# Routing attention and a tanh-shrink feed-forward: scores as [key, query], two heads on two halves of the array, masks by codes

## The chip, the core and the metric

One core of a Trainium2 chip. The metric is device time in microseconds of one execution of the program, from the first to the last instruction; of several runs the median counts.

## The reference

There are 4 batches, 8 heads, 768 tokens and 64 dimensions per head. Each token of q and of k is given one of 16 clusters of its head, and a query attends only to the keys of its own cluster. The attention's output, [3072 tokens, 512], goes through an up-projection to 2048, h - tanh(h), and a down-projection to 512.

```python
q_assign = np.argmax(np.einsum('bhsd,hcd->bhsc', q_n, c_n), axis=-1)   # k_assign alike
mask = q_assign[:, :, :, None] == k_assign[:, :, None, :]
scores = scale * np.matmul(q, k.transpose(0, 1, 3, 2))
scores = np.where(mask, scores, -1000000000.0)
scores = scores - np.max(scores, axis=-1, keepdims=True)
attn = np.exp(scores)
attn = attn / (np.sum(attn, axis=-1, keepdims=True) + 1e-09)
x = np.matmul(attn, v)            # then heads side by side: (3072, 512)
h = x @ w_in
out = (h - np.tanh(h)) @ w_out
```

q, k, v and the centroids are float32 normals times 0.1. The two weights come as float64 and are rounded to float32 on the chip. All arithmetic is float32.

## The kernel before

The 32 heads (4 batches x 8) are worked on one after the other, g = 0 to 31. The 768 tokens of a head stand as 6 chunks of 128 partitions.

For one head, `turn` (L185) transposes q and k from [token, d] to [d, token] on TensorE, 12 transposes `pt`. `route` (L201) multiplies each chunk with the 16 centroids (`pr`, 12 thin products of 16 columns), takes the argmax on VectorE as a one-hot row, transposes it (`po`) and puts it under the turned q, and (one-hot - 1) x 2^60 under the turned k. So one product over 64 + 16 rows gives the masked score: `score` (L237) does it for one chunk of 128 queries against 768 keys, two products of 384 columns. `softmax` (L245) takes the row's maximum on VectorE (L248), the exponential with its sum on ScalarE (L251), and scales by the reciprocal on VectorE (L256). `turn_weights` (L258) transposes the 128x768 weights in six 128x128 transposes (`pw`, L267) and ScalarE copies them out (L269). `values` (L271) multiplies v with the turned weights of half a head's queries, six products `av` (L279), into rows 0 to 63 or 64 to 127 of `xT` by the head's parity.

The projections (`ffn_items`, L287) work on half a batch, 384 tokens. There are 16 items `up` (four products `h` of 384 columns, L296, a tanh on ScalarE, L301, and a subtraction `g` on VectorE, L302) and 12 items `project` (four products `o` of 512 columns, L308). The items of a finished batch are spread over the next batch's eight heads by `step` in the main loop: they are issued between a head's chunks. Those of the last batch follow at the end. A float32 product is issued as two instructions of TensorE, each with a weight load of its own; a transpose is one instruction.

Weights are loaded in 32 pieces by GpSimd's queue (L111) and rounded by six VectorE operations and one GpSimd addition each (L115 to L134), four pieces per head of batch 0. Loads of q, k and v are on SP's queue (L183), two heads ahead, with 1536 bytes in a row per partition. The centroids' load (L147) is the fourth on that queue. The output's stores are on GpSimd's queue (L315).

The order on each engine is that of a scheduler, which starts from the order in which the program issues the work. PSUM has eight banks: two score tiles of two banks (`ps_s`), two for transposes (`ps_t`), two for `av`, `h` and `o` (`ps_f`).

Of the kernel before, what the change touches and what calls it, by code (L numbers as in the profile page):

```python
# [26 lines left out]
BF16 = mybir.dt.bfloat16  # L27
U32 = mybir.dt.uint32
# [7 lines left out]
TINY = 1e-30  # L36


@with_exitstack
def kernel(  # L40
# [11 lines left out]
    PSUM = bass.MemoryType.PSUM  # L52

# [5 lines left out]
    NG = B * H  # L59
    KR = D + C  # L60
# [7 lines left out]
    assert H * C == P and 2 * D == P and H * D == DM  # L68

    const = ctx.enter_context(tc.tile_pool(name="const", bufs=1))  # L70
    loads = ctx.enter_context(tc.tile_pool(name="loads", bufs=3))
    xtp = ctx.enter_context(tc.tile_pool(name="xtp", bufs=2))
    rtp = ctx.enter_context(tc.tile_pool(name="rtp", bufs=2))
    expp = ctx.enter_context(tc.tile_pool(name="expp", bufs=3))
# [26 lines left out]
    def load_weights(n: int):  # L101
# [4 lines left out]
        if words == 1:  # L106
            nc.gpsimd.dma_start(dst, src)
            return
# [30 lines left out]
    def constants():  # L139
        make_identity(nc, ident)  # L140
        nc.vector.tensor_copy(out=identb, in_=ident)
        for c in range(C):
            nc.vector.memset(down[:, c : c + 1], float(C - c))
# [216 lines left out]
    for it in fill:  # L360
        it()
# [31 lines left out]
```

## Time and profile before

| | |
|---|---|
| median of three runs | 1651.25 us (1644.41 to 1651.29) |
| span of the profiled execution | 1650.8 us |
| TensorE busy | 1565.0 us, 95% |
| VectorE / ScalarE / GpSimd busy | 702.1 / 464.0 / 78.5 us |
| products and transposes of TensorE, busy | `o` 362.1, `h` 357.5, `sc` 311.1, `av` 276.4, `pw` 173.5, `pr` 101.7, `pt` 54.8, `po` 32.3 us |

The engines work in parallel, and busy time is each engine's own. The span is the profiled execution from its first to its last instruction; runs are timed without the profiler. A matmul's recorded duration contains its way through the array, which overlaps the next one's, so the pace of a group is read from the start of the group to the start of the next. The granted clock is the share of 2.4 GHz that TensorE was given over a stretch; its two levels are 1.2 and 2.4 GHz.

### The profile page before, as it was taken

What the parts mean: (1) busy time and instruction counts of PE and PEld (TensorE: products, weight loads), DVE (VectorE), ACT (ScalarE), POOL (GpSimd) and SP (SyncE); (2) the same over time, 40 slices, a digit from 0 to 9 for tenths busy, and PEclk for the clock granted to TensorE, in tenths of its full rate; (3) what the DMA queues carried; (4) which work ended last, traced back from release to release, by engine and by line L of the source; (5) the groups of instructions that cost most, each with busy time, mean ns of one, the idle gap of its engine ahead of it and who ended that gap; (6) DMA issues with size and microseconds to landing.
All of it is one profiled execution on the core that took longest, in us unless ns stands there. A gap on an engine that the chain in (4) does not pass through costs nothing.

```text
span 1650.8 us, 15280 instructions
## 1 busy us (share of the span) xinstructions
PE 1565.0 (95%) x6017; PEld 880.4 (53%) x6017; DVE 702.1 (43%) x1463; ACT 464.0 (28%) x995; POOL 78.5 (5%) x94
## 2 busy tenths in 40 slices
PE   4788788899999999999999999999999999999998
PEld 2444445556555555555555555556655566545453
DVE  6857675544433444334433444334443344321010
ACT  1223333433322333223322333223322233221010
POOL 3312220000000000000000000000000000000000
PEclk9877787989999999999999999999999999999999
DMA  4212210000000000000000000000000000000000
GB/s 169 90 55 74 70 53 15 29 15 15 15 17 11 22 15 15 24 24 15 12 10 21 21 15 15 21 27 3 13 15 27 21 15 1 7 13 0 19 0 19
DMA packets 20567, 42.96 MB, mean 26 GB/s; under 512 B 2576, under 2 KB 14864, under 8 KB 20496
## 3 DMA queue, kind: packets, MB, share of 16 engines
q0 software_dynamic: 6528, 23.07, 4.2%
q1 hardware_dynamic: 13968, 18.91, 3.7%
q8 instruction: 48, 0.79, 0.2%
q14 instruction: 23, 0.19, 0.0%
HBM read 35.68 MB, written 6.29 MB: 25 GB/s over the span
## 4 chain that ended last, share of the span: by engine, by line
issue 70%; PE 19%; DVE 7%; ACT 2%; POOL 1%; DMA 0%; POOLq 0%; ACTq 0%
PE av L279 5%; PE sc L240 4%; PE pw L267 3%; PE pr L206 3%; PE h L296 3%; DVE raw L130 1%; PE o L308 1%; DVE top L248 1%; ACT e L251 1%; POOL out_dram L315 1%; ACT eT L269 1%; DVE rest L126 1%; PE po L225 1%; PE pt L192 1%; DVE e L256 0%
## 5 line engine op out<-in xcount | busy, mean ns | idle before, releaser
L308 PE MATMUL o<-w_out,g 128*128 128x512 f32 x768 | 362.1, 619 | 0.0
L296 PE MATMUL h<-xT,w_in 128*128 128x384 f32 x1024 | 357.5, 495 | 0.0
L240 PE MATMUL sc<-xqk 80*128 80x384 f32 x768 | 311.1, 518 | 19.4 <-ACT e L251 18.1
L251 ACT ACTIVATE e<-sc,top 128x768 f32<-128x768 f32 x192 | 173.1, 902 | 483.5 <-DVE top L248 478.1
L279 PE MATMUL av<-eT,x 128*64 128x384 f32 x768 | 276.4, 511 | 0.9 <-ACT eT L269 0.2
L296 PEld LDWEIGHTS h<-xT,w_in 128*128 128x128 f32 x1024 | 193.1, 193 | 128.7 <-issue 6.6
L248 DVE TENSOR_REDUCE top<-sc 128x1 f32<-128x768 f32 x192 | 183.2, 956 | 144.1 <-PE sc L240 144.0
L308 PEld LDWEIGHTS o<-w_out,g 128*128 128x128 f32 x768 | 147.3, 196 | 163.4 <-issue 151.6
L269 ACT COPY eT<-pw 128x384 f32<-128x384 f32 x384 | 167.2, 483 | 216.6 <-PE pw L267 216.0
L267 PEld LDWEIGHTS pw<-ident,e 128*128 128x128 f32 x1152 | 142.8, 148 | 101.5 <-issue 58.8
L279 PEld LDWEIGHTS av<-eT,x 128*64 128x64 f32 x768 | 103.5, 142 | 161.4 <-issue 127.3
L267 PE MATMUL pw<-ident,e 128*128 128x128 f32 x1152 | 173.5, 288 | 14.8 <-DVE xqk L199 4.7
L240 PEld LDWEIGHTS sc<-xqk 80*128 80x128 f32 x768 | 133.0, 199 | 101.7 <-issue 41.4
L282 DVE COPY xT<-av 64x384 f32<-64x384 f32 x64 | 35.5, 555 | 295.2 <-PE av L279 295.1
L301 ACT ACTIVATE th<-h 128x384 f32<-128x384 f32 x128 | 63.1, 493 | 253.0 <-PE h L296 250.4
L256 DVE TENSOR_SCALAR e<-e,rec 128x768 f32<-128x768 f32 x192 | 121.0, 630 | 5.7
L302 DVE TENSOR_TENSOR g<-h,th 128x384 f32<-128x384 f32 x128 | 71.4, 558 | 118.3 <-ACT th L301 110.9
L206 PEld LDWEIGHTS pr<-cnT,xqk 64*128 64x128 f32 x768 | 98.5, 206 | 18.6 <-ACT eT L269 18.2
L206 PE MATMUL pr<-cnT,xqk 64*128 64x16 f32 x768 | 101.7, 275 | 1.5 <-ACT eT L269 1.5
L315 POOL DMA_DIRECT2D out_dram<-osb x24 | 13.0, 544 | 1372.3 <-DVE osb L314 1372.3
L228 ACT CAST xqk<-po 16x768 f32<-16x768 bf16 x32 | 25.3, 790 | 162.6 <-PE po L225 162.6
L253 DVE TENSOR_SCALAR den<-total 128x1 f32<-128x1 f32 x192 | 29.0, 151 | 89.6 <-ACT e L251 84.6
(52 smaller groups left out, 581.0 us busy)
## 6 DMA issues: line engine op xcount, KB each, us to landing
raw<-in_moe_w_in_dram POOLq DMA_DIRECT2D x16, 512.0 KB, 4.7
raw<-in_moe_w_out_dram POOLq DMA_DIRECT2D x16, 512.0 KB, 3.9
x<-in_q_dram SPq DMA_DIRECT2D x32, 192.0 KB, 2.4
x<-in_k_dram SPq DMA_DIRECT2D x32, 192.0 KB, 2.5
x<-in_v_dram SPq DMA_DIRECT2D x32, 192.0 KB, 3.1
out_dram<-osb POOLq DMA_DIRECT2D x24, 256.0 KB, 2.3
cen<-in_centroids_dram SPq DMA_DIRECT2D x1, 32.0 KB, 6.3
```

What stands on the lines that cost most here:

```text
L206: nc.tensor.matmul(pr[:, j], lhsT=x[0:D, j], rhs=cnT[:, g % H], start=True, stop=True)
L240: nc.tensor.matmul(sc[:, half, 0:TB], lhsT=xqk[g][:, 0, i], rhs=xqk[g][:, 1, half * HCH : (half + 1) * HCH], start=True, stop=True,)
L248: nc.vector.tensor_reduce(out=top, in_=sc, axis=AX.XY, op=ALU.max, negate=True)
L251: nc.scalar.activation(out=e, in_=sc, func=ACT.Exp, bias=top, scale=1.0, accum_out=total)
L256: nc.vector.tensor_scalar_mul(out=e, in0=e, scalar1=rec)
L267: nc.tensor.transpose(out=pt[:, j], in_=e[:, c * P : (c + 1) * P], identity=ident)
L269: nc.scalar.copy(out=dst, in_=pt)
L279: nc.tensor.matmul(av[r], lhsT=x32[g][:, 2, j], rhs=eT[:, j], start=(j == 0), stop=(j == NCH - 1))
L296: nc.tensor.matmul(h, lhsT=w_in[i][:, c, o * P : (o + 1) * P], rhs=xT[b][:, c, half * TB : (half + 1) * TB], start=(c == 0), stop=(c == CD ...
L301: nc.scalar.activation(out=th, in_=h, func=ACT.Tanh)
L302: nc.vector.tensor_tensor(out=gs[i][:, o], in0=h, in1=th, op=ALU.subtract)
L308: nc.tensor.matmul(acc[sub], lhsT=gs[i][:, o, sub * P : (sub + 1) * P], rhs=w_out[i][:, o], start=(i == 0 and o == 0), stop=(i == NQ4 - 1 ...
```

## The change

The kernel's working part is rewritten as `fast()`, issued under a schedule written by hand (`tc.manual_schedule()`), so that each engine's order is the program's.

- Heads go in pairs (16 pairs). q and k of two heads are loaded side by side, [128, 6, 2, 64], so each transpose turns both heads: head 0 lands on partitions 0 to 63, head 1 on 64 to 127.
- `similar` multiplies both heads with a block-diagonal of their centroids (32 columns), four products of 384 columns into four strips of 32 partitions; `route` turns the result in three transposes and finds each token's code (16 minus its cluster's number) by four VectorE operations; `publish` turns the queries' codes to rows and stores them in DRAM; `spread` loads them back onto all 128 partitions.
- `score` gives [key, query] for one chunk of 128 keys and 384 queries of both heads: two products of 64 rows, head 0 on rows 0 to 63, head 1 on 64 to 127, into two PSUM banks. ScalarE takes the exponential in place, without a maximum. `select` on VectorE multiplies it with (query's code == key's code), which gives the weights as [key, query], with nothing to turn.
- `value` multiplies v with the weights, head 0 into output partitions 0 to 63, head 1 into 64 to 127. GpSimd adds the weights up, `total` sums them over the keys by a product with ones, and `divide` takes reciprocals and scales.
- A step is two key chunks of a pair and half of the queries; a pair and half has three steps, a block (half a batch) four pairs, twelve steps; there are eight blocks. The projections of block n - 1 are issued among the steps of block n, 28 items over 12 steps, those of block 7 at the end. Block 0 has none. One piece of weights is rounded per step in block 0 and three per step in block 1, with four VectorE operations, one on ScalarE and one on GpSimd.
- If any sum of weights lies outside 2^-5 to 2^80, a flag sends the program on to `general()`, which computes everything again as before, without overlap. It is left out below.
- The output's copies move from VectorE to ScalarE and its stores from GpSimd's queue to SP's.

```diff
...
+    def fast():
...
+        loads = cx.enter_context(tc.tile_pool(name="loads", bufs=2))
+        vp = cx.enter_context(tc.tile_pool(name="vp", bufs=4))
+        codep = cx.enter_context(tc.tile_pool(name="codep", bufs=5))
+        qbp = cx.enter_context(tc.tile_pool(name="qbp", bufs=3))
+        ep = cx.enter_context(tc.tile_pool(name="ep", bufs=2))
+        ps_s = cx.enter_context(tc.tile_pool(name="ps_s", bufs=2, space=PSUM))
+        ps_a = cx.enter_context(tc.tile_pool(name="ps_a", bufs=2, space=PSUM))
+        ps_f = cx.enter_context(tc.tile_pool(name="ps_f", bufs=2, space=PSUM))
...
+        def round_weights(n: int):
...
+            nc.scalar.activation(out=rest, in_=lo, func=ACT.Copy, scale=2.0**-29)
...
+            nc.gpsimd.tensor_tensor(out=rest, in0=bits, in1=rest, op=ALU.add)
+            nc.vector.tensor_scalar(
+                out=bits, in0=hi, scalar1=20, scalar2=0x7FF,
+                op0=ALU.logical_shift_right, op1=ALU.bitwise_and,
+            )
+            nc.vector.scalar_tensor_tensor(
+                out=dst, in0=bits, scalar=float(F32_LEAST), in1=rest.bitcast(F32),
+                op0=ALU.is_ge, op1=ALU.mult,
+            )
...
+        def load(n: int, what=(0, 1)):
...
+                for h in range(2):
+                    nc.sync.dma_start(
+                        t[:, :, h], (q, k, v)[i][b, 2 * p + h].rearrange("(p j) d -> p j d", p=P)
+                    )
+        def turn(n: int):
+            for i in range(2):
+                pt = ps_s.tile([P, 2, 512], F32, name="pt", tag="s")
+                x = raw_qk.pop((n, i))
+                for j in range(NCH):
+                    nc.tensor.transpose(
+                        out=pt[:, j // HCH, (j % HCH) * P : (j % HCH + 1) * P],
+                        in_=x[:, j].rearrange("p h d -> p (h d)"), identity=ident,
+                    )
...
+        def similar(n: int):
+            for i in range(2):
+                for half in range(2):
+                    r = (2 * i + half) * 2 * C
+                    nc.tensor.matmul(
+                        ps[r : r + 2 * C, 0, 0:TB], lhsT=bd[:, pairs[n][1]],
+                        rhs=turned[n, i][:, half], start=True, stop=True, tile_position=(0, r),
+                    )
+            t = rtp.tile([P, TB], F32, name="simt")
+            nc.scalar.copy(out=t, in_=ps[:, 0, 0:TB])
...
+        def route(n: int):
+            ps, t = sims.pop(n)
+            for j in range(HCH):
+                nc.tensor.transpose(
+                    out=ps[:, 1, j * P : (j + 1) * P], in_=t[:, j * P : (j + 1) * P], identity=ident
+                )
...
+            nc.vector.reduce_max(out=mx, in_=pr, axis=AX.X)
...
+            nc.vector.tensor_tensor(out=top, in0=top, in1=places, op=ALU.mult)
+            code = codes[n] = codep.tile([P, 2, 2, 2, HCH], F32, name="code")
+            nc.vector.reduce_max(
+                out=code.rearrange("p i a h j -> p j (i a h)"),
+                in_=top.rearrange("p (j g) c -> p j g c", j=HCH), axis=AX.X,
+            )
...
+        def publish(n: int):
+            ps, code = sims.pop(n)
+            G = HCH * 4
+            nc.tensor.transpose(
+                out=ps[0:G, 0, 0:P], in_=code[:, 0].rearrange("p a h j -> p (a h j)"), identity=ident
+            )
+            t = rtp.tile([G, P], F32, name="qc")
+            nc.vector.tensor_copy(out=t, in_=ps[0:G, 0, 0:P])
+            q_codes[n] = dram.tile([2, 2, HCH, P], F32, name="q_codes")
+            nc.sync.dma_start(q_codes[n].rearrange("a h j p -> (a h j) p"), t)
+        rows = {}
+        def spread(n: int, half: int):
+            t = rows[n, half] = qbp.tile([P, 2, TB], F32, name="row")
+            nc.sync.dma_start(
+                t.rearrange("p h n -> p (h n)"),
+                q_codes[n][half].rearrange("h j p -> (h j p)").unsqueeze(0).to_broadcast([P, 2 * TB]),
+            )
+        def score(n: int, half: int, j: int):
+            sc = scores[n, half, j] = ps_s.tile([P, 2, 512], F32, name="sc", tag="s")
+            for h in range(2):
+                r = slice(h * D, h * D + D)
+                nc.tensor.matmul(
+                    sc[:, h, 0:TB],
+                    lhsT=turned[n, 1][r].rearrange("p a n -> p (a n)")[:, j * P : (j + 1) * P],
+                    rhs=turned[n, 0][r, half], start=True, stop=True,
+                )
+            nc.scalar.activation(out=sc[:, :, 0:TB], in_=sc[:, :, 0:TB], func=ACT.Exp, scale=SCALE)
+        def select(n: int, half: int, j: int):
+            if j % 2 == 0:
+                weights[n, half, j // 2] = ep.tile([P, 2, 2, TB], F32, name="e")
+            e = weights[n, half, j // 2][:, j % 2]
+            sc = scores.pop((n, half, j))
+            for h in range(2):
+                nc.vector.scalar_tensor_tensor(
+                    out=e[:, h], in0=rows[n, half][:, h],
+                    scalar=codes[n][:, 1, j // HCH, h, j % HCH : j % HCH + 1], in1=sc[:, h, 0:TB],
+                    op0=ALU.is_equal, op1=ALU.mult,
+                )
+            if j % 2 == 1:
+                pair = weights[n, half, j // 2]
+                if j == 1:
+                    s = sums[n, half] = sump.tile([P, 2, TB], F32, name="sum")
+                    nc.gpsimd.tensor_tensor(out=s, in0=pair[:, 0], in1=pair[:, 1], op=ALU.add)
+                else:
+                    s = sums[n, half]
+                    for i in range(2):
+                        nc.gpsimd.tensor_tensor(out=s, in0=s, in1=pair[:, i], op=ALU.add)
+        def value(n: int, half: int, s: int):
+            e = weights.pop((n, half, s))
+            if s == 0:
+                avs[n, half] = ps_a.tile([P, TB], F32, name="av", tag="a")
+            for i in range(2):
+                j = 2 * s + i
+                for h in range(2):
+                    nc.tensor.matmul(
+                        avs[n, half][h * D : h * D + D], lhsT=vals[n][:, j, h], rhs=e[:, i, h],
+                        start=(j == 0), stop=(j == NCH - 1),
+                    )
+        dens = {}
+        def total(n: int, half: int):
+            b, p = pairs[n]
+            s = sums.pop((n, half))
+            ps = ps_a.tile([P, TB], F32, name="den", tag="a")
+            for h in range(2):
+                nc.tensor.matmul(
+                    ps[h * D : h * D + D], lhsT=ones, rhs=s[:, h], start=True, stop=True
+                )
+            if p == 0:
+                xT[b, half] = xp.tile([P, CD, TB], F32, name="xT")
+            nc.scalar.copy(out=xT[b, half][:, p], in_=avs.pop((n, half)))
+            t = dens[n, half] = sump.tile([P, TB], F32, name="den")
+            nc.scalar.activation(out=t, in_=ps, func=ACT.Copy, bias=EPS)
+            is_in = okp.tile([P, TB], F32, name="is_in")
+            for bound, op in ((SUM_LEAST, ALU.is_ge), (SUM_MOST, ALU.is_le)):
+                nc.gpsimd.tensor_scalar(out=is_in, in0=t, scalar1=bound, scalar2=None, op0=op)
+                nc.gpsimd.tensor_tensor(out=ok, in0=ok, in1=is_in, op=ALU.mult)
+        def divide(n: int, half: int, part: int):
+            b, p = pairs[n]
+            c = slice(part * P, (part + 1) * P)
+            t = dens[n, half]
+            nc.vector.reciprocal(out=t[:, c], in_=t[:, c])
+            if part == HCH - 1:
+                x = xT[b, half][:, p]
+                nc.vector.tensor_tensor(out=x, in0=x, in1=dens.pop((n, half)), op=ALU.mult)
...
+        load(0)
+        constants()
+        load(0, (2,))
+        load(1)
+        for n in range(1, HP):
+            load(n, (2,))
+        centroid_norms()
+        for n in range(2):
+            fetch_weights(n)
+        fetched, rounded = 2, 0
...
+        def prepare(n: int, stage: int):
+            if n >= len(pairs):
+                return
+            if stage == 0:
+                turn(n)
+                load(n + 2)
+            elif stage == 1:
+                similar(n)
+            elif stage == 2:
+                route(n)
+            elif stage == 3:
+                publish(n)
+                spread(n, 0)
+        for stage in range(4):
+            prepare(0, stage)
+        begin(steps[0])
+        for i in range(2):
+            select(*steps[0][:2], i)
+        fill, late = [], []
+        for at, (n, half, s) in enumerate(steps):
+            b, p = pairs[n]
+            following = steps[at + 1] if at + 1 < len(steps) else None
+            if p == 0 and s == 0:
+                block = 2 * b + half
+                fill = ffn_items((block - 1) // 2, (block - 1) % 2) if block else []
+            left = HP * NS - (p * NS + s)
+            now = [fill.pop(0) for _ in range(-(-len(fill) // left))]
+            nxt = n + 1 if half == 0 and p + 1 < HP else (b + 1) * HP if half == 1 and p + 1 == HP else None
+            if nxt is not None and s == NS - 1:
+                prepare(nxt, 3)
+            if following:
+                begin(following)
+            value(n, half, s)
+            if s == NS - 1:
+                total(n, half)
+                late += [lambda n=n, half=half, i=i: divide(n, half, i) for i in range(HCH)]
+                if half == 1:
+                    load(n + HP, (2,))
+            todo = []
+            if following:
+                todo += [lambda i=i: select(*following[:2], 2 * following[2] + i) for i in range(2)]
+            todo += late
+            late = []
+            if block <= 1:
+                todo += [weights_on] * (1 if block == 0 else 3)
+            pre = [lambda: None] * 4
+            if nxt is not None:
+                pre = [lambda st=st: prepare(nxt, st) for st in range(4)]
+            if half == 1 or (half == 0 and p == HP - 1):
+                m = b * HP + p + 1 if half == 1 and p + 1 < HP else b * HP if half == 0 else None
+                if m is not None and s == 0:
+                    spread(m, 1)
+            slots = max(len(now), 1)
+            for i in range(slots):
+                mine = todo[i * len(todo) // slots : (i + 1) * len(todo) // slots]
+                def between(mine=mine):
+                    for it in mine:
+                        it()
+                if i < len(now):
+                    now[i](between)
+                else:
+                    between()
+                if i == max(slots - 2, 0):
+                    if s == 0:
+                        pre[0]()
+                    elif s == 1:
+                        pre[1]()
+                if i == slots - 1 and s == 1:
+                    pre[2]()
+        fill = ffn_items(B - 1, 1)
+        for it in late:
+            it()
+        for it in fill:
+            it(lambda: None)
...
+    fine = nc.values_load(flag[0:1, 0:1], min_val=0, max_val=1)
+    with tc.If(fine < 1):
+        with ExitStack() as cx:
+            general()
```

## Rows read from the trace of the kernel before

**Rows 1.** The page's list of busy time.
```profile
PE 1565.0 (95%) x6017; PEld 880.4 (53%) x6017; DVE 702.1 (43%) x1463; ACT 464.0 (28%) x995; POOL 78.5 (5%) x94
```

**Rows 2.** Stretches: us; PE, PEld, DVE, ACT, POOL busy; clock, DMA share, GB/s.
```profile
0.00:20.00 20.00, 6.14 (x28) 4.66 (x28) 8.12 (x40) 2.45 (x4) 5.52 (x13) 1.00 0.69 240
38.10:358.00 319.90, 264.14 (x1056) 154.26 (x1057) 211.58 (x440) 101.01 (x216) 53.01 (x50) 0.80 0.17 53
100.00:200.00 100.00, 79.41 (x307) 47.28 (x306) 67.25 (x143) 28.07 (x60) 22.03 (x22) 0.74 0.22 65
455.00:1475.00 1020.00, 1019.76 (x4030) 570.81 (x4028) 400.37 (x825) 305.33 (x659) 9.79 (x18) 0.98 0.05 16
1475.00:1651.00 176.00, 168.77 (x459) 85.99 (x457) 22.57 (x39) 15.71 (x32) 3.25 (x6) 0.99 0.03 11
810.02:814.49 4.47, 4.47 (x10) 2.17 (x9) 1.78 (x5) 0.48 (x1) 0.00 (x0) 0.62 0.00 0
```

**Rows 3.** Timeline of TensorE in the filled stage: start, duration, then the group.
```profile
801.97 1.46 PE L240 MATMUL sc<-xqk 80*128 80x384 f32 x4
803.26 2.75 PE L296 MATMUL h<-xT,w_in 128*128 128x384 f32 x8
805.84 0.82 PE L267 MATMUL pw<-ident,e 128*128 128x128 f32 x6
806.50 0.81 PE L296 MATMUL h<-xT,w_in 128*128 128x384 f32 x2
807.24 2.85 PE L206 MATMUL pr<-cnT,xqk 64*128 64x16 f32 x24
810.02 4.54 PE L296 MATMUL h<-xT,w_in 128*128 128x384 f32 x8
814.49 0.84 PE L225 MATMUL po<-identb,oh 128*16 128x128 bf16 x12
815.25 2.20 PE L296 MATMUL h<-xT,w_in 128*128 128x384 f32 x6
...
817.95 0.81 PE L240 MATMUL sc<-xqk 80*128 80x384 f32 x2
818.69 4.08 PE L279 MATMUL av<-eT,x 128*64 128x384 f32 x12
822.70 2.20 PE L240 MATMUL sc<-xqk 80*128 80x384 f32 x6
...
1447.19 3.60 PE L308 MATMUL o<-w_out,g 128*128 128x512 f32 x8
1450.63 0.82 PE L267 MATMUL pw<-ident,e 128*128 128x128 f32 x6
```

**Rows 4.** Groups by line and shape: count, then busy us, mean ns of one.
```profile
L240 PE MATMUL sc<-xqk 80*128 80x384 f32 x768 | 311.1, 518 | 19.4 <-ACT e L251 18.1 <-DVE xqk L230 1.1
L251 ACT ACTIVATE e<-sc,top 128x768 f32<-128x768 f32 x192 | 173.1, 902 | 483.5 <-DVE top L248 478.1 <-DVE den L253 4.8 <-DVE rec L255 0.6
L302 DVE TENSOR_TENSOR g<-h,th 128x384 f32<-128x384 f32 x128 | 71.4, 558 | 118.3 <-ACT th L301 110.9
L130 DVE TENSOR_SCALAR raw<-raw 128x512 uint32<-128x512 uint32 x32 | 28.7, 903 | 0.1
L129 POOL TENSOR_TENSOR rest<-w_in,rest 128x512 f32<-128x512 f32 x16 | 23.2, 1452 | 72.2 <-DVE rest L126 59.4 <-DVE rec L255 12.8
L122 DVE TENSOR_SCALAR raw<-w_in 128x512 uint32<-128x512 uint32 x16 | 6.6, 418 | 0.0
```

**Rows 5.** DMA issues: size of one, median us from issue to landing.
```profile
x<-in_q_dram SPq DMA_DIRECT2D x32, 192.0 KB, 2.4
```

**Rows 6.** Timeline of the start, VectorE and ScalarE.
```profile
8.41 0.23 DVE L150 TENSOR_TENSOR sq<-cen 128x64 f32<-128x64 f32 x1
...
38.10 0.90 ACT L251 ACTIVATE e<-sc,top 128x768 f32<-128x768 f32 x1 [8.50 <-DVE top L248]
```

**Rows 7.** Timeline of the end, VectorE.
```profile
1643.81 0.69 DVE L314 COPY osb<-o 128x512 f32<-128x512 f32 x1 [13.04 <-PE o L308]
```

More of the change, by code (lines that the diff above doesn't have):

```diff
@@ L36 @@
 TINY = 1e-30
+EPS = 1e-9
+SUM_LEAST = 2.0**-5
+SUM_MOST = 2.0**80
 @with_exitstack
@@ L173, in centroid_norms, with general @@
+    def general():
+        xd = dram.tile([B, DM, S], F32, name="xd")
+        gs = cx.enter_context(tc.tile_pool(name="gs", bufs=1))
+        gps = cx.enter_context(tc.tile_pool(name="gps", bufs=1, space=PSUM))
+        identb = gs.tile([P, P], BF16, name="identb")
+        nc.vector.tensor_copy(out=identb, in_=ident)
+        cnT = gs.tile([D, H, C], F32, name="cnT")
+        pc = gps.tile([D, P], F32, name="pc", tag="t")
         nc.tensor.transpose(out=pc, in_=cn, identity=ident)
         nc.vector.tensor_copy(out=cnT.rearrange("d h c -> d (h c)"), in_=pc)
-    x32, xqk = {}, {}
@@ L179, in load @@
-    def load(g: int):
-        b, h = g // H, g % H
-        x32[g] = loads.tile([P, 3, NCH, D], F32, name="x32")
-        for i, src in enumerate((q, k, v)):
-            nc.sync.dma_start(x32[g][:, i], src[b, h].rearrange("(p j) d -> p j d", p=P))
-    def turn(g: int):
-        xqk[g] = xtp.tile([KR, 2, NCH, P], F32, name="xqk")
-        for i in range(2):
-            for half in range(2):
-                pt = ps_t.tile([D, HCH, P], F32, name="pt", tag="t")
-                for j in range(HCH):
-                    nc.tensor.transpose(
-                        out=pt[:, j], in_=x32[g][:, i, half * HCH + j], identity=ident
-                    )
-                dst = xqk[g][0:D, i, half * HCH : (half + 1) * HCH]
-                if i == 0:
-                    nc.scalar.mul(out=dst, in_=pt, mul=SCALE)
-                else:
-                    nc.vector.tensor_copy(out=dst, in_=pt)
@@ L258, in turn_weights @@
-    def turn_weights(g: int, i: int):
-        half = i // HCH
-        if i % HCH == 0:
-            turned[g, half] = etp.tile([P, NCH, HCH, P], F32, name="eT")
-        e = weights.pop((g, i)).rearrange("p a n -> p (a n)")
-        for part in range(2):
-            pt = ps_t.tile([P, HCH, P], F32, name="pw", tag="t")
-            for j in range(HCH):
-                c = part * HCH + j
-                nc.tensor.transpose(out=pt[:, j], in_=e[:, c * P : (c + 1) * P], identity=ident)
-            dst = turned[g, half][:, part * HCH : (part + 1) * HCH, i % HCH]
-            nc.scalar.copy(out=dst, in_=pt)
@@ L271, in values @@
-    def values(g: int, half: int):
-        b, h = g // H, g % H
-        if h == 0 and half == 0:
-            xT[b] = xp.tile([P, CD, S], F32, name="xT")
-        eT = turned.pop((g, half)).rearrange("k j a n -> k j (a n)")
-        r = slice((h % 2) * D, (h % 2) * D + D)
-        av = ps_f.tile([P, TB], F32, name="av", tag="f")
-        for j in range(NCH):
-            nc.tensor.matmul(
-                av[r], lhsT=x32[g][:, 2, j], rhs=eT[:, j], start=(j == 0), stop=(j == NCH - 1)
-            )
-        nc.vector.tensor_copy(out=xT[b][r, h // 2, half * TB : (half + 1) * TB], in_=av[r])
@@ L322 @@
-    load(0)
-    constants()
-    centroid_norms()
-    load(1)
-    turn(0)
-    route(0)
-    fill = []
-    for g in range(NG):
-        if g + 2 < NG:
-            load(g + 2)
-        if g < H:
-            for n in range(g * len(PIECES) // H, (g + 1) * len(PIECES) // H):
-                load_weights(n)
-        n = -(-len(fill) // (H - g % H))
-        now = [fill.pop(0) for _ in range(n)]
-        def step(m: int, of: int):
-            for it in now[m * n // of : (m + 1) * n // of]:
-                it()
-        score(g, 0)
-        softmax(g, 0)
-        for i in range(NCH):
-            if i + 1 < NCH:
-                score(g, i + 1)
-                softmax(g, i + 1)
-            elif g + 1 < NG:
-                route(g + 1)
-            step(i, NCH)
-            turn_weights(g, i)
-            if i == 1 and g + 1 < NG:
-                turn(g + 1)
-            if i % HCH == HCH - 1:
-                values(g, i // HCH)
-        if g % H == H - 1:
-            for half in range(2):
-                fill += ffn_items(g // H, half)
```

443 lines of the change are left out of this document (280 added, 163 removed).

## The prediction

> **What bounds the kernel now.** I read four views in this order. First the page's list of busy time: TensorE is busy 1565 us of 1650.8, VectorE 702, ScalarE 464, GpSimd 78 [rows 1]. Then the same by stretch: up to 358 us (the eight heads of batch 0, with no projections among them) TensorE is not full and its clock is at 0.80 of 2.4 GHz; from there to 1475 us it is busy without a gap (0.98 in the 1020 us shown); the tail of 176 us is the last batch's projections alone [rows 2]. So from 358 us on, a microsecond of TensorE work is a microsecond of time, and before that latency and the weights' rounding count. Third, the timeline of TensorE in the filled stage, where a group's pace is the distance to the next group's start, over its count. Fourth, the groups by line, for durations on the other engines.
>
> The pace at full clock: an instruction of 384 columns takes 0.3225 us (four of `sc` 1.29, eight of `h` 2.58), one of 512 columns 0.429, a 128x128 float32 transpose 0.11, a group of 24 `pr` 2.78, twelve `po` 0.76, twelve `av` 4.01 [rows 3]. A float32 product is two instructions (768 for 384 products of `sc` [rows 4]), a transpose one.
>
> So one head costs 1.3 (12 `pt`, transposes too) + 2.8 (`pr`) + 0.8 (`po`) + 7.7 (24 `sc`) + 4.0 (36 `pw`) + 8.0 (24 `av`) = 24.6 us, 32 heads 787; the projections 1024 x 0.3225 + 768 x 0.429 = 660. Together 1447 us; the other 204 are mostly the first 358 us, where eight heads take 40 us each instead of 24.6.
>
> **What the change takes from TensorE.** I count per pair of heads and half of the queries (a "pair-half", the size of one head before; 32 of them, four to a block, eight blocks).
> - The 36 weight transposes are gone: 4.0 us per head, and with them 384 copies on ScalarE. `pr` and `po` go too: 3.6 us.
> - `turn`: 12 transposes serve two heads, so 0.65 us per pair-half. `similar` is four products (8 instructions) per pair, `route` three transposes, `publish` one.
> - `score` and `value` keep their count, 12 products (24 instructions of 384 columns) each per pair-half; `total` adds two.
>
> **The term that decides** is what two neighbouring products cost when one uses rows 0 to 63 and the next 64 to 127 (`score`, into two PSUM banks), or columns 0 to 63 and 64 to 127 (`value`, `total`). The trace has no such neighbours: its half-array products (`av`, 64 columns) run many in a row on the same half, at the full 0.334 us an instruction [rows 3]. Upper bound: no overlap, 2.58 us for a step's four `score` products. Lower bound: all overlap, 1.29. The two products have no row or column of the array, no weights and no output in common, and TensorE already takes in one instruction while the last one drains (the eight `h` run on 0.17 us after the next group has begun [rows 3]), so I take overlap. But a product's two instructions go one after the other on the same half, so overlap is between the second of one product and the first of the next: A1, A2 with B1, B2 with C1, C2 with D1, D2: five slots instead of eight, 1.61 us.
>
> The Trainium skill ("TensorEngine Tiling (Array Packing)", Key Properties) says that tiles on different parts of the array load weights and multiply in parallel; with all of it the step would be the lower bound. No run so far shows it for float32.
>
> Against it stands a cost that the trace does show: going into `av` and out of it takes 0.24 us beyond the pace (0.74 instead of 0.645 before it, 4.01 instead of 3.87 in it) [rows 3]. Each step now goes full, rows, columns, full: three changes of 0.12, 0.36 us.
>
> One pair-half, then: score 3 x 1.61, value 3 x 1.61, total 0.97, changes 1.1: 11.7 us. Preparation per pair: turn 1.3, similar 1.9, route and publish 0.4: 3.6.
>
> **The wait it adds.** `route` is issued last in a step and `publish` first in the next, so TensorE's queue meets the transpose of the codes right after the route's transposes, and everything stands behind it: the next scores, values and fill. It waits for four VectorE operations of 384 columns, 0.56 each (the size of `g`, 558 ns [rows 4]), and for a `g` ahead of them: 3 us, 15 times. The old `po` waited for the one-hot too, but projections stood between.
>
> A block with projections: fill 660/8 = 82.4; four pair-halves 46.9; two preparations 13.2 with their waits; 2 for `total`, which waits for the last two sums on GpSimd. That is 144.5, at the clock of 0.98 [rows 2] 147 us.
>
> **Other engines, per pair-half of some 36 us.** VectorE: 12 selects of 0.56 = 6.7, `g` 2.2, three reciprocals of 128 columns (0.19 each at `g`'s pace is the lower bound, eight times that, 1.5, the upper; I take 1.1, since nothing hangs on it) and a product, 3.8, half a preparation 1.7: 15. ScalarE: 6 exponentials of 0.9 [rows 4], copies and tanh: 10. GpSimd: a float32 addition of 512 columns takes 1.45 [rows 4], so five additions of 768 are 10.7 and the bound tests up to 4.3: 15. None is near 36; their cost is nothing as long as TensorE's 36 cover it, and the excess if blocks get shorter. The output's stores move from GpSimd's queue to SP's, where they stand among the loads half a batch ahead: nothing. Publishing and spreading the codes is two transfers of at least 2.4 us each, as a load of 192 KB [rows 5]; VectorE waits in the next select, under 7 us of TensorE work.
>
> **The start.** The centroids' load is now behind 16 loads of 192 KB rather than 3, and those land in pieces of 256 bytes rather than 1536. The old one lands at 8.4 us [rows 6]. 3.1 MB at the 240 GB/s of the first 20 us [rows 2] is 13 us; at one sixth of that, 78. I take 25, nearer the first, since the first packets went at full rate. Then norms 8 (6 before), similarity, route, codes 5, two transfers 5: first select at 45 us, against a first exponential at 38.1 [rows 6].
>
> **Block 0** has no fill and is a loop of latencies: per pair-half VectorE has 19 us including three rounded weight pieces; each piece's last two operations wait for GpSimd's addition, which stands behind sums of 2.1 each. Bounds: 19 (VectorE alone) and 40 (a head now). I take 29: 115 us. In the old kernel the operation beside GpSimd's addition takes 903 ns where its like takes 420 [rows 4].
> The Trainium skill ("GPSIMD Engine Reference", Specifications) says that the two engines share SBUF interfaces when VectorE has two SBUF inputs or uses two ports, which agrees with that row; were every reciprocal held up by one addition, block 0 would be 24 us longer and the sum 1334.
>
> **Block 1** rounds the other 20 pieces, three per step: VectorE 144 us of work and waits beside TensorE's 147. I add 28.
>
> **The tail** is one half block rather than two: 82.4/0.99, then 7.0 us from the last copy to the end as now [rows 7], and 3 for the flag and the branch: 93.
>
> **Sum:** 45 + 115 + 175 + 6 x 147 + 93 = 1310. The profiled execution spans 1650.8 us and the median is 1651.25, so the sum stands for both. A measurement of this kernel tells about 0.5% from no change.
>
> **The rivals.**
> 1. *The halves don't overlap* (the change does not do what its name says). For it: the only half-array products in the trace run at the full pace. A pair-half is then 17.9 us and a block 169, at 0.98 172: 45 + 115 + 186 + 1034 + 93 = 1473. Faster still, by transposes and `pr` alone.
> 2. *Only one of the two kinds overlaps,* rows or columns: midway, 1395.
> 3. *The clock falls, slower than before.* In the old trace, after 24 thin products of 16 columns the next eight `h` take 4.47 us instead of 2.58, at a clock of 0.62, that is, most of it at 1.2 of 2.4 GHz; and from 100 to 200 us, with TensorE 79% busy, the clock is 0.74 [rows 2, 3]. If the waits for codes and for VectorE make blocks 1 to 7 like that stretch, their 1039 us stretch: 253 + 1039/c. It decides from c = 0.74; at 0.70 it is 1737. Against it: 3 us waits come only 15 times, and 82 us of dense projections per block are spread over all steps.
> 4. *The second part runs.* It repeats everything if a sum leaves 2^-5 to 2^80. The inputs give every cluster 26 to 72 keys and scores within 0.06 of zero, so sums near 24 to 77: excluded in practice.
>
> **Chances.** Overlap 0.58 (own range 1230 to 1400), one kind 0.12, none 0.22, the clock or another wait making it slower 0.05, within 0.5% 0.02, something else faster 0.01. Faster 0.93, same 0.02, slower 0.05. The range reaches down to a short start and block 0 (1200) and up over most of the case without overlap (1510).
>
> **What would show it.** Overlap: in the timeline four `score` products (8 instructions) start within 1.6 us rather than 2.6, `value` alike. The wait: TensorE idle 2 to 4 us before the codes' transpose, 15 times, for VectorE's last maximum. Block 0 ends near 160 us, block 1 near 335, then blocks 147 apart. Wrong would be VectorE or GpSimd busy over 80% in blocks 2 to 7, or a clock under 0.9 there.

## The result, and the profile after

The changed kernel takes 1258.06 us, the median of four runs (1256.86 to 1260.11), against 1651.13 of the kernel before beside it: a ratio of 0.763, 95% interval 0.761 to 0.765. The forecast was 1310, with the range from 1200 to 1510. The profiled execution took 1258.72 us and spans 1256.9. Its page has, beside [rows 1]:

```profile
PE 1084.5 (86%) x3842; PEld 503.2 (40%) x3842; DVE 530.5 (42%) x902; ACT 294.4 (23%) x475; POOL 486.7 (39%) x358
```

TensorE lost 480 us of work. By stretch, with the columns of [rows 2], these are block 0, block 1 and blocks 2 to 7; the last row is a short stretch of block 3:

```profile
39.70:177.80 138.10, 76.92 (x296) 30.68 (x296) 89.76 (x129) 35.33 (x52) 75.27 (x59) 0.73 0.26 74
177.80:349.90 172.10, 139.00 (x459) 62.98 (x457) 105.09 (x172) 43.35 (x73) 91.19 (x77) 0.91 0.28 84
349.90:1167.10 817.20, 776.48 (x2834) 362.45 (x2833) 317.89 (x542) 199.94 (x323) 318.24 (x215) 0.99 0.11 30
650.00:656.00 6.00, 4.97 (x19) 2.04 (x21) 1.22 (x3) 1.66 (x3) 0.00 (x0) 0.72 0.25 66
```

From 350 us on TensorE is the bound (95% busy, clock 0.99); before, it is not. Set beside the forecast:

| | forecast | measured |
|---|---|---|
| to the first select | 45 | 39.7 |
| block 0 | 115 | 138.1 |
| block 1 | 175 | 172.1 |
| blocks 2 to 7 | 882 | 817.2 |
| tail | 93 | 89.8 |

The two large differences are of opposite sign: -65 and +23. The timeline of TensorE in the filled stage, read as [rows 3] by the distance from start to start, shows the first:

```profile
604.27 0.85 PE L251 MATMUL sim<-t,bd 128*32 128x384 f32 x8
605.05 3.70 PE L406 MATMUL o<-w_out,g 128*128 128x512 f32 x8
...
611.57 0.28 PE L287 MATMUL sim<-ident,code 128*12 128x128 f32 x1 [2.49 <-DVE code L278]
611.77 1.56 PE L312 MATMUL sc<-t,t 64*128 64x384 f32 x8
613.26 1.51 PE L348 MATMUL av<-e,vals 128*64 128x384 f32 x8
614.60 0.81 PE L361 MATMUL den<-sum,ones 128*64 128x384 f32 x4
615.35 7.13 PE L406 MATMUL o<-w_out,g 128*128 128x512 f32 x16
622.41 1.56 PE L312 MATMUL sc<-t,t 64*128 64x384 f32 x8
623.90 1.51 PE L348 MATMUL av<-e,vals 128*64 128x384 f32 x8
625.35 5.43 PE L393 MATMUL h<-xT,w_in 128*128 128x384 f32 x16
```

Four `score` products, eight instructions of 384 columns, give way to the next group after 1.49 us, four `value` products after 1.45 (622.41 to 623.90 to 625.35). Eight instructions in a row would be 2.58. With 0.12 for a change of the array's use, as forecast, 2.94 for the step is eight slots of 0.3225 and three changes: four slots where I had counted five. The timeline from 622.30 to 622.43 us has two instructions of the group that begins at 622.41, so they started within 0.02 us of each other:

```profile
622.41 0.59 PE L312 MATMUL sc<-t,t 64*128 64x384 f32 x2
```

The view doesn't say which products they belong to. But instructions on one half do not overlap (`same_half` below), so two that start together lie on different halves: A1 runs with B1 and A2 with B2, and nothing waits half a product. `similar`, four strips of 32 columns, does its eight instructions in 0.78 us. The list of waits (us in all, times, longest) shows the wait that the change added:

```profile
PE sim L287 <- DVE code L278: 48.7, 16, 4.4
```

The wait for the codes is 48.7 / 16 = 3.04 us each; forecast was 3.0. VectorE waits for the codes' rows up to 6.7 us, which the forecast had put under 7 us of TensorE work. Not foreseen were the reciprocals' waits for GpSimd's bound tests. VectorE by line, as [rows 4]:

```profile
L326 DVE SCALAR_TENSOR_TENSOR e<-row,code,sc 128x384 f32<-128x384 f32 x384 | 213.2, 608 | 229.6 <-ACT sc L317 99.8 <-DMA row<-q_codes 70.8 <-issue 46.8
L378 DVE RECIPROCAL den<-den 128x128 f32<-128x128 f32 x96 | 83.3, 917 | 57.1 <-POOL is_in L371 57.1
```

The select takes 0.61 (0.56 forecast), the reciprocal 0.92 (1.1 taken, bounds 0.19 and 1.5) after 57.1 us of waits, an addition of 768 columns on GpSimd 1.81 (2.1).

Block 0, where the other difference lies, in the timeline of GpSimd and VectorE:

```profile
44.88 3.79 POOL L339 TENSOR_TENSOR sum<-sum,e 128x768 f32<-128x768 f32 x2 [1.07 <-DVE e L326]
```

```profile
45.93 1.08 DVE L147 TENSOR_SCALAR w_in<-raw 128x512 uint32<-128x512 uint32 x1
47.04 2.18 DVE L151 SCALAR_TENSOR_TENSOR w_in<-raw,w_in 128x512 uint32<-128x512 uint32 x1
...
50.66 0.43 DVE L155 TENSOR_SCALAR w_in<-raw 128x512 uint32<-128x512 uint32 x1 [1.44 <-POOL rest L154]
51.12 0.69 DVE L159 SCALAR_TENSOR_TENSOR w_in<-w_in,rest 128x512 f32<-128x512 uint32 x1
```

L151 and L159 are the same operation on the same size, with two inputs in SBUF (L151 reads every second word of one; `two_phase` below shows that this is not the cause). L159, with GpSimd at rest, takes 0.69 us; L151, started while GpSimd adds up weights, takes 2.18. Of the eleven pieces whose rounding starts in block 0, eight have an L151 of 2.18 and three, with GpSimd at rest, one of 0.69. An operation with one input is held up, too: L147 takes 1.08 beside the additions, L155, of the same form, 0.43 behind them.

### The profile page after: what moved, and what is told of

The parts are those of the page before. It is cut to its first block, busy times and chain, and to the rows that moved or that the text cites. A ratio compares the mean times of both kernels' runs of the same rounds, so it can differ in the third digit from the quotient of the medians.

```text
span 1256.9 us, 10657 instructions
## 1 busy us (share of the span) xinstructions
PE 1084.5 (86%) x3842; PEld 503.2 (40%) x3842; DVE 530.5 (42%) x902; ACT 294.4 (23%) x475; POOL 486.7 (39%) x358
## 4 chain that ended last, share of the span: by engine, by line
PE 76%; DVE 14%; POOL 5%; ACT 1%; issue 1%; DMA 1%; SPq 1%; POOLq 0%; DVEq 0%; ACTq 0%
PE o L406 26%; PE h L393 24%; PE sc L312 11%; PE av L348 10%; POOL rest L154 3%; DVE w_in L151 2%; DVE e L326 2%; PE pt L233 2%; PE den L361 2%; SPq L223 1%; DVE den L378 1%; POOL is_in L371 1%; PE sim L251 1%; DVE w_in L147 1%; DVE w_out L151 1%
## 5 line engine op out<-in xcount | busy, mean ns | idle before, releaser
L339 POOL TENSOR_TENSOR sum<-sum,e 128x768 f32<-128x768 f32 x128 | 232.1, 1813 | 348.9 <-DVE e L326 346.4
L326 DVE SCALAR_TENSOR_TENSOR e<-row,code,sc 128x384 f32<-128x384 f32 x384 | 213.2, 608 | 229.6 <-ACT sc L317 99.8
L317 ACT ACTIVATE sc<-sc 128x768 f32<-128x768 f32 x192 | 145.9, 793 | 271.2 <-PE sc L312 270.6
L312 PE MATMUL sc<-t,t 64*128 64x384 f32 x768 | 173.4, 571 | 37.0 <-DVE e L326 23.3
L371 POOL TENSOR_SCALAR is_in<-den 128x384 f32<-128x384 f32 x64 | 75.0, 1171 | 222.0 <-ACT den L368 219.0
L348 PE MATMUL av<-e,vals 128*64 128x384 f32 x768 | 158.3, 537 | 0.0
L312 PEld LDWEIGHTS sc<-t,t 64*128 64x128 f32 x768 | 73.3, 206 | 123.2 <-issue 74.7
L378 DVE RECIPROCAL den<-den 128x128 f32<-128x128 f32 x96 | 83.3, 917 | 57.1 <-POOL is_in L371 57.1
L335 POOL TENSOR_TENSOR sum<-e 128x768 f32<-128x768 f32 x32 | 57.8, 1806 | 40.2 <-DVE e L326 40.2
L372 POOL TENSOR_TENSOR ok<-ok,is_in 128x384 f32<-128x384 f32 x64 | 63.8, 997 | 5.3
L287 PE MATMUL sim<-ident,code 128*12 128x128 f32 x16 | 5.1, 320 | 48.7 <-DVE code L278 48.7
```

What stands on the lines that cost most here:

```text
L312: nc.tensor.matmul(sc[:, h, 0:TB], lhsT=turned[n, 1][r].rearrange("p a n -> p (a n)")[:, j * P : (j + 1) * P], rhs=turned[n, 0][r, half], ...
L317: nc.scalar.activation(out=sc[:, :, 0:TB], in_=sc[:, :, 0:TB], func=ACT.Exp, scale=SCALE)
L326: nc.vector.scalar_tensor_tensor(out=e[:, h], in0=rows[n, half][:, h], scalar=codes[n][:, 1, j // HCH, h, j % HCH : j % HCH + 1], in1=sc[: ...
L339: nc.gpsimd.tensor_tensor(out=s, in0=s, in1=pair[:, i], op=ALU.add)
L348: nc.tensor.matmul(avs[n, half][h * D : h * D + D], lhsT=vals[n][:, j, h], rhs=e[:, i, h], start=(j == 0), stop=(j == NCH - 1),)
L371: nc.gpsimd.tensor_scalar(out=is_in, in0=t, scalar1=bound, scalar2=None, op0=op)
```

## The experiments

**Do the halves overlap, and what is it worth?** Three kernels put the products of head 1 on the rows, the columns, or both, of head 0.

`same_half` has both edits (those of `same_rows` and `same_cols` below).

> Both heads' scores take rows 0 to 63 (head 1's scores are computed from head 0's data), and all value products but one per pair-half go to columns 0 to 63, so that neighbours can't overlap; count, columns and order stay. Theory (the overlap is worth its face value): four score products 2.58 us instead of 1.29, four value products nearly as much, 84 to 96 steps of each that TensorE bounds: 1475 to 1505 us. Rival (other engines would bound the steps anyway, the gain is the removed transposes): under 1300.

It took 1497.3 us, one run. The timeline of TensorE, the window of its blocks 2 to 7, and a short one within them:

```profile
655.50 2.85 PE L312 MATMUL sc<-t,t 64*128 64x384 f32 x8
658.27 2.79 PE L349 MATMUL av<-e,vals 128*64 128x384 f32 x8
661.00 4.56 PE L407 MATMUL o<-w_out,g 128*128 128x512 f32 x10
```

```profile
388.40:1405.70 1017.30, 976.56 (x2833) 457.77 (x2833) 320.85 (x542) 205.59 (x323) 318.04 (x215) 0.95 0.09 24
761.30:771.40 10.10, 9.50 (x15) 4.00 (x16) 1.96 (x4) 1.59 (x2) 0.00 (x0) 0.50 0.10 40
```

The same instructions take 2.77 and 2.73 us. Of the 200 us by which blocks 2 to 7 are longer, 72 steps x 1.29 for `score` and, for `value`, 24 pair-halves x (0.65 + 2 x 1.29) are 170; in a pair-half's first step the edit leaves one product on the other columns. The rest, 30, goes with the clock of 0.95 instead of 0.99. The low clock stands around the waits for the codes: one of them ends at 761.9 us, and the clock is 0.50 from 761.3 to 771.4. Block 7, which has no such wait, has a clock of 1.00, though its products stay on one half as well.

```diff
-                r = slice(h * D, h * D + D)
+                r = slice(0, D)
```

> Only the scores on one half (head 1's scores are computed from head 0's data). Theory: 1366 to 1382 us. Rival (only the column halves overlap): 1258. In the timeline eight score instructions take 2.6 us instead of 1.5.

`same_rows` took 1402.2, one run, above the expected range. Its blocks 2 to 7 took 936.5 us at a clock of 0.95: +119, of which 93 are counted and some 26 are the clock, which I had left out of the expectation.

```diff
+                    up = j == 0 and h == 1
                     nc.tensor.matmul(
-                        avs[n, half][h * D : h * D + D], lhsT=vals[n][:, j, h], rhs=e[:, i, h],
-                        start=(j == 0), stop=(j == NCH - 1),
+                        avs[n, half][up * D : up * D + D], lhsT=vals[n][:, j, h], rhs=e[:, i, h],
+                        start=(j == 0), stop=up or (j == NCH - 1 and h == 1),
```

> Only the value products on one half (head 1's values are added onto head 0's). Theory: 1358 to 1375 us. Rival (only the row halves overlap): 1258. With the run before, the two costs add up to that of both together if TensorE alone bounds the steps.

`same_cols` took 1346.3, one run, below the expected range, since I had not counted the product that still overlaps (2.08 us to the next group in a pair-half's first step; 2.73 in the others). The timeline, and the window of its blocks 2 to 7:

```profile
616.57 2.15 PE L349 MATMUL av<-e,vals 128*64 128x384 f32 x8
618.65 3.70 PE L407 MATMUL o<-w_out,g 128*128 128x512 f32 x8
```

```profile
356.39:1254.72 898.33, 857.60 (x2833) 395.82 (x2833) 318.43 (x542) 200.11 (x323) 318.09 (x215) 0.98 0.10 27
```

These blocks are 81 us longer, of which 78 are counted as above; their clock, 0.98, is nearly the changed kernel's.

Rows and columns overlap alike, and their costs nearly add: the spans are 143 and 88 us above the changed kernel's, both together 238. The overlap is the larger part of the gain: with hardly any of it 1497 of 1651 is left, with it 1258.

**What does the rounding of the weights cost?** `one_copy` replaces its six instructions by a copy.

```diff
-            nc.scalar.activation(out=rest, in_=lo, func=ACT.Copy, scale=2.0**-29)
...
+            nc.vector.tensor_copy(out=dst.bitcast(U32), in_=hi)
```

> The weights' rounding is left out (one copy of the high words takes its place), the loads stay. Theory (blocks 0 and 1 are bound by VectorE and its waits for GpSimd in the rounding): block 0 falls from 138 to about 95 us and block 1 from 172 to about 146, in all 1190 us. Rival (block 0 is bound by the chain of score, exponential, select and the sums on GpSimd): 1235 or more.

1179.1 us, one run. Its blocks 0 and 1:

```profile
39.70:134.20 94.50, 65.64 (x297) 26.74 (x297) 59.57 (x93) 28.18 (x40) 57.62 (x45) 0.84 0.38 108
134.20:268.70 134.50, 128.00 (x458) 58.76 (x456) 66.42 (x111) 32.94 (x53) 67.91 (x59) 0.99 0.34 107
```

Block 0 is 43.6 us shorter (43 expected), block 1 37.6 (26 expected): the rounding costs the 80 us between the spans, though in the changed kernel VectorE is busy only 65% of block 0.

**What covers the wait for the codes?** `value_first` issues the step's `value` between `route` and `publish` instead of behind the next scores.

```diff
-            if nxt is not None and s == NS - 1:
+            first = nxt is not None and s == NS - 1
+            if first:
+                value(n, half, s)
...
-            value(n, half, s)
+            if not first:
+                value(n, half, s)
```

> In a pair's last step the value products are issued ahead of the codes' transpose rather than behind it. Theory (TensorE stands still for 3.0 us there, 16 times, for VectorE's last maximum): 1.44 us of value products fit into 15 of these waits: 22 us less, 1236 us, ratio to the changed kernel 0.983. Rival (the scores that follow start no earlier, and the wait only moves to the next exponential): 1258.

1225.73 us (1223.71 to 1229.03), ratio 0.741 (0.739 to 0.743): -32, more than the theory's -22. TensorE, and the window of blocks 2 to 7:

```profile
591.42 1.51 PE L348 MATMUL av<-e,vals 128*64 128x384 f32 x8
593.98 0.28 PE L287 MATMUL sim<-ident,code 128*12 128x128 f32 x1 [1.05 <-DVE code L278]
```

```profile
339.30:1132.10 792.80, 767.31 (x2834) 357.81 (x2833) 316.31 (x542) 197.37 (x323) 318.23 (x215) 1.00 0.11 31
```

All waits for codes together fall from 48.7 to 26.8 us, the 22 of the theory. The other 10 is a second price of the wait: in blocks 2 to 7 TensorE's busy time for the same 2834 instructions falls from 776.5 to 767.3 us. In the changed kernel TensorE after a wait in block 3:

```profile
651.03 0.28 PE L287 MATMUL sim<-ident,code 128*12 128x128 f32 x1 [3.08 <-DVE code L278]
651.24 2.50 PE L312 MATMUL sc<-t,t 64*128 64x384 f32 x8
653.67 2.22 PE L348 MATMUL av<-e,vals 128*64 128x384 f32 x8
655.72 0.81 PE L361 MATMUL den<-sum,ones 128*64 128x384 f32 x4
```

The scores take 2.43 us and the values 2.05, where 1.49 and 1.45 are usual; the granted clock from 650 to 656 us is 0.72, so part of it ran at 1.2 GHz, after 3.08 us without work. That is 1.5 us on top of 3.1. Not every wait was followed by it, and its length alone does not decide: the one of 2.49 us at 611.57 was not, nor one of 3.08 us at 690.4 (clock 1.00 to 696), but one of 2.49 us at 887.2 was (0.71 to 893). With waits of 1.05 and 1.64 us, the clock of blocks 2 to 7 is 1.00.

`split` issues the next step's first score, too, ahead of the codes.

```diff
+            if nxt is not None and s == NS - 1 and following:
+                score(*following[:2], 2 * following[2])
+                value(n, half, s)
                 prepare(nxt, 3)
+                score(*following[:2], 2 * following[2] + 1)
```

> In a pair's last step one score chunk of the next step and the value products are issued ahead of the codes' transpose, the other score chunk behind it. Theory (with the value products ahead 1.05 us of wait is left, 15 times): 0.9 us of scores fit in, less a change of array use: 8 to 12 us less than with the value products alone, 1214 to 1218. Rival (what the first move gave beyond 1.44 us per wait was the clock, and no low clock is left after block 1 to regain; the rest of the wait lies on VectorE's chain and moves with it): 1223 or more.

1221.08 us, ratio 0.739 (0.736 to 0.742): -4.7 against `value_first`, between the two.

```profile
594.02 0.28 PE L287 MATMUL sim<-ident,code 128*12 128x128 f32 x1 [0.20 <-DVE code L278]
594.67 0.92 PE L312 MATMUL sc<-t,t 64*128 64x384 f32 x4 [0.37 <-DVE qc L291]
```

The wait is 0.20, but the second score now waits 0.37 for VectorE's copy of the codes (its tile reuses that bank), and the split groups change the array's use twice more.

**Do the reciprocals, behind GpSimd's bound tests, cost block 0 its time?** `own_rec` writes them to a tile of their own, so that the tests need not be done before.

```diff
-            nc.vector.reciprocal(out=t[:, c], in_=t[:, c])
+            t, rec = dens[n, half], recs[n, half]
+            nc.vector.reciprocal(out=rec[:, 0, c], in_=t[:, c])
```

> The reciprocals go to a tile that is no longer used (the sums), not over the sums' row that GpSimd's four bound tests still read. Theory (VectorE waits 57 us for those tests, and in blocks 0 and 1 that is on the path): 10 to 25 us less, 1233 to 1248. Rival (VectorE has slack, the next wait is GpSimd's addition): 1255 to 1260.

1258.44 us, ratio 0.760 (0.758 to 0.762): no change. The chain of waits in block 0, here and then at the same place in the changed kernel:

```profile
65.66 3.13 DMA row<-q_codes
...
68.92 2.19 DVE e L326 x4
71.11 2.50 DVE sum L378 x3
...
75.36 2.18 DVE w_in L151
...
80.12 2.10 DVE e L326 x4
```

```profile
73.84 2.59 DVE den L378 x3
...
77.43 0.70 DVE w_in L151
...
80.71 1.57 DVE e L326 x3
```

The reciprocals, now behind selects that wait for the codes' rows on their way over DRAM, start 2.7 us sooner, but the next selects only 0.6. The rounding moves up with the reciprocals and now runs beside a GpSimd addition: L151 takes 2.18 us where it took 0.70. All eleven pieces of block 0 are held up so, eight before, and VectorE is busy 97.7 us in block 0 instead of 89.8. Most of what the waits gave back, the hold-up took; neither the theory nor the rival had that.

**The start.** `cen_first` moves the centroids' load ahead of the 16 loads.

```diff
+        cen = const.tile([P, D], F32, name="cen")
+        nc.sync.dma_start(cen, centroids.rearrange("h c d -> (h c) d"))
```

> The centroids' load is issued first on SP's queue rather than 17th. Theory (the first select waits for the centroids, which land at 20.9 us): first select near 28 instead of 39.7 us, 10 to 12 us less, 1247. Rival (the loads of q and k in pieces of 256 bytes land no earlier than 20 us and set the start): 1256 or more.

1248.11 us, ratio 0.754 (0.752 to 0.756): -10. In the changed kernel the norms begin with the first of these rows:

```profile
20.88 0.23 DVE L178 TENSOR_TENSOR sq<-cen 128x64 f32<-128x64 f32 x1 [19.33 <-DMA cen<-in_centroids_dram]
```

Here the codes are there at 17.8, but their transfer is issued behind loads on SP's queue, at 20.8, and that of the rows at 24.4 (timelines of VectorE and of SP's queue):

```profile
17.49 0.28 DVE L289 COPY qc<-sim 12x128 f32<-12x128 f32 x1 [0.37 <-PE sim L285]
27.96 2.19 DVE L324 SCALAR_TENSOR_TENSOR e<-row,code,sc 128x384 f32<-128x384 f32 x4 [10.19 <-DMA row<-q_codes]
```

```profile
19.06 1.67 SPq L221 DMA_DIRECT2D x<-in_k_dram  x2
20.83 0.83 SPq L291 DMA_DIRECT2D q_codes<-qc  x1
```

**VectorE's wait for GpSimd within a rounded piece.** `two_phase` ends `round_weights` after GpSimd's addition and does the last two operations at the next piece.

```diff
+            halfway[n] = dst, bits, hi, rest
+        def finish_weights(n: int):
...
-                round_weights(rounded)
...
+                finish_weights(rounded - 1)
...
+                    round_weights(rounded)
```

> A weight piece's last two VectorE operations are issued with the next piece, so that VectorE doesn't wait for GpSimd's addition between them (48 us of waits in all). Theory: 24 us less in block 0 and 10 to 20 in block 1: 1215 to 1225. Rival (GpSimd, with its sums and additions, sets the pace there; VectorE's wait only moves): 1250 or more.

1233.24 us, ratio 0.745 (0.743 to 0.747): -25, short of the forecast. Block 0 took 120.6 us and block 1 165.0. By line, the last operation of a piece (ns: least, median, most):

```profile
L165 DVE SCALAR_TENSOR_TENSOR w_in<-w_in,rest x16: 691/2175/2184, 53.2 to 187.9; 128x512 f32<-128x512 uint32 x16
```

The operation that took 0.69 in the changed kernel now takes 2.18, since it now runs beside additions, and the median of L151 has fallen to 0.69: the hold-up moved from one to the other. It belongs to the pairing in time, not to the line or to how the line reads.

**All together.** `joined` has `value_first`, `own_rec`, `cen_first` and `two_phase`; `joined3` has `split` in place of `value_first`; `joined2` is `joined3` with a piece of weights ahead of the selects in the last step of each pair-half of block 0.

> Value products ahead, reciprocals to their own place, centroids first, rounding in two phases, together. Theory (they act on different stretches: the waits for codes, the start, blocks 0 and 1): the single gains add up, 32 + 0 + 10 + 25: 1191, give or take 8. Rival (the rounding and the waits for codes share block 0's path): 1205 or more.

1187.08 us, ratio 0.718 (0.715 to 0.721): as the single gains add up.

> The same with the scores split around the codes' transpose. Theory: 8 to 12 us less than the run before: 1181. Rival: the same as it, 1191.

1183.57 us, ratio 0.716 (0.713 to 0.719): 3.5 less.

```diff
-            if block <= 1:
-                todo += [weights_on] * (1 if block == 0 else 3)
+            if block == 0:
+                todo = [weights_on] + todo if s == NS - 1 else todo + [weights_on]
```

> The same again, and in block 0's steps before a new pair the weight piece is issued ahead of the selects, which wait there for the codes' row from DRAM (4 to 7 us). Theory (that wait ends last once the bound tests are off the path): three to four such steps, 2 us of rounding in each: 6 to 8 us less: 1174. Rival (the selects are late instead by the piece): 1181 or more.

1185.34 us, ratio 0.717 (0.714 to 0.720): nothing gained, as the rival had it. `joined3` beats both kernels: 0.94 of the changed one's time. By stretch, as above:

```profile
28.00:139.00 111.00, 70.80 (x297) 27.18 (x297) 88.65 (x127) 34.54 (x52) 71.62 (x56) 0.81 0.31 87
139.00:302.10 163.10, 136.69 (x459) 61.35 (x457) 111.66 (x174) 44.16 (x74) 95.56 (x80) 0.92 0.30 91
302.10:1091.80 789.70, 770.05 (x2835) 356.96 (x2834) 318.40 (x542) 198.45 (x323) 318.70 (x215) 1.00 0.11 31
```

The 75 us between the spans are 11.7 of the start, 27.1 of block 0, 9.0 of block 1 and 27.5 of blocks 2 to 7. The last stretch is 98% TensorE work at full clock. In blocks 0 and 1 TensorE is still idle for 67 of 274 us.

## Why the prediction was right

**The mechanism holds.** The halves overlap, and `same_half` shows what the first rival would have been: 1497 us (1473 forecast). Only one kind would have been 1346 or 1402 (1395). The 1473 has 14 us for block 1's rounding, where the forecast has 28, and gives no reason; with 28 it is 1487. The reason given for the overlap needs a correction: the two products have no cell of the array in common, but `score`'s two share all columns and `value`'s all rows. That the sum came within 52 us is partly luck, since -65 and +23 cancel in part.

**The step that failed is "five slots instead of eight, 1.61 us".** It had a product of one half start with the second instruction of the other. The traces show the pairs starting together, four slots, and my lower bound of 1.29 with the changes of use (0.12 each) that I had added. That takes 0.65 off each step's 3.58, and 0.23 off `total`'s 0.97.
The Trainium skill ("TensorEngine Tiling (Array Packing)", Key Properties) says that different tiles load weights and multiply in parallel; the 1.49 us of the trace agree, for float32 too.

Blocks 2 to 7 by these: without preparations I had (144.5 - 13.2) / 0.98 = 134 us for a block; by window, the blocks with three preparations took 146.5 us and those with one 130, so a preparation is 8.2 and the rest 122 (block 7, without a preparation and without a next block's first scores, took 118). Of these 12 us, 7.8 are the steps, 0.9 `total`'s products, 2 its wait, for which the timeline has nothing, and 1.3 the clock of 0.99. The preparation, forecast at 6.7 with the clock, came out at 8.2, although `similar` was 1.1 shorter: its low clock after the wait, and a wait of 0.9 in `turn` for ScalarE's copy of the first six transposes, I had not counted.

**Block 0 was mis-sized the other way,** 34.5 us per pair-half for my 29. Of the 23 us, 14 are VectorE's own work (89.8 us busy, where I had 4 x 19 = 76), 9 its waits. I had seen the hold-up beside GpSimd in [rows 4] (903 ns for 420), but charged it as a mere possibility to the reciprocals. They were not held up (0.92); the rounding was: L151 in eight pieces, 8 x (2.18 - 0.69) = 12 us, and L147 in five of them, 4 us. That these 16 lay wholly on the path was not shown; `two_phase`, which took away the waits within a piece and only moved the hold-up, made block 0 17.5 us shorter.
The Trainium skill ("GPSIMD Engine Reference", Specifications) names VectorE's instructions with two SBUF inputs, and those in a two-port mode, as the ones that contend for the shared interface. L151 (2.18 us) agrees, and so does the reciprocal (0.92), which has one input. L147 and the operation in [rows 4] have one input, too, and were held up; whether they run in such a mode no run here shows.

**Block 1** came out right, but as a sum: a shorter base and a dearer rounding (172.1 against a filled block's 130 with one preparation, 42 where I added 28).

**The start** was 5 us shorter: the loads in pieces of 256 bytes brought the centroids at 20.9 rather than 25 (the terms written there, 25, 8, 5 and 5, add up to 43, not 45). **The wait for codes** was right in size, and only its consequence for the clock was missed. **The other engines** cost nothing in blocks 2 to 7, as forecast (VectorE and GpSimd busy 39%). **The third rival** fell: clock 0.99 there, and 0.91 in block 1. **The fourth** did not occur: the program ends with its flag.

## What to carry to other kernels

Two float32 products on two halves of the array, issued in turn, cost one: count both instructions of the pair as started together, and add about 0.12 us for each change between full array, row halves and column halves. A wait of TensorE for a few small operations of another engine is best filled with products that are already released; that gave back the wait and the low clock after it. Before handing additions to GpSimd, see which VectorE operations will run beside them; a change that removes a wait can move them there, as `own_rec` did.

## What was not expected of the hardware

- Instructions on two halves start within 0.02 us of each other; four strips of 32 columns do eight instructions of 384 columns in 0.78 us.
- Kernels whose `score` products stay on one row half had a lower granted clock with TensorE as busy: 0.95 in blocks 2 to 7 of `same_half` and `same_rows`, 96% busy, against 0.99 at 95%. `same_cols`, whose `value` products stay on one column half, had 0.98. In `same_half` the low clock stood around the waits for the codes, 10 us at the one shown; why so long is open.
- Beside GpSimd's additions a SCALAR_TENSOR_TENSOR of 128x512 with two inputs in SBUF took 2.18 us instead of 0.69, in either of two lines, and a TENSOR_SCALAR with one input 1.08 instead of 0.43. The selects, with one of two inputs in PSUM, took 0.60 to 0.62 throughout.
- 3.08 us without work were followed by products at 1.2 GHz, 1.5 us on top, but not every time.
